# Attention with 16-wide heads: scores and maxima as fp32r pairs in the two row halves of the array, heads streamed in groups of three, TensorE order written out

## The chip, the cores and the metric

The kernel runs on one core of a Trainium2 chip. The metric is the device time of one execution in microseconds (us). The core has TensorE (PE in the profile; PEld is its weight load), VectorE (DVE), ScalarE (ACT), GpSimd (POOL) and SyncE (SP, which only issues DMAs). TensorE writes to PSUM, which has eight banks of 128 x 512 fp32. SBUF is the working memory.

## The reference

Two layers, each made of an attention block and an MLP with Mish, on 2048 tokens of width 512. There are 32 heads of width 16, so the scores of one layer are 32 matrices of 2048 x 2048.

```python
B, S, D, H = 1, 2048, 512, 32
Dh = D // H
q, k, v = qkv[0], qkv[1], qkv[2]
scores = jnp.einsum("bhqd,bhkd->bhqk", q, k) * (Dh ** -0.5)
p = _softmax(scores, axis=-1)
o = jnp.einsum("bhqk,bhkd->bhqd", p, v)
...
x = x + _A_ref(_layernorm(x, axis=-1), A_wqkv, A_wo)
x = x + _B_ref(_layernorm(x, axis=-1), B_w1, B_b1, B_w2)
x = x + _A_ref(_layernorm(x, axis=-1), A_wqkv, A_wo)
x = x + _B_ref(_layernorm(x, axis=-1), B_w1, B_b1, B_w2)
```

## The kernel before

**Stages.** For each layer: layernorm and transposition (`norm_parts`), the projections to q, k and v (`qkv`), the attention (`Attention.run`), the output projection (`wo_parts`), and the MLP (`mlp`). Matmuls with full precision are made of three fp32r matmuls on a high and a low part (`mm3`, L111).

**q and k.** `qkv` splits each 128 x 512 piece of the projected q or k into three bf16 parts (L385 to L388: ACT, DVE, ACT, POOL) and stores them to a scratch tensor in DRAM, with a DMA that ACT issues. `prep_qk` (L187) loads them for a group of four heads, from SP's queue: 16 partitions for each of six products of a part of k with a part of q, so that one matmul over 96 rows gives the score in nearly full precision. Two more rows (to 98) carry ones in k and the negated row maximum in q, so that the score comes out with the maximum already subtracted.

**The attention.** A group has four heads, and a layer eight groups. A group runs over four blocks of 512 queries, and a block over 16 key tiles of 128; a step `s` is one key tile of one block for four heads. There are 512 steps in a layer. In a step:

- `score` (L273), four times: one matmul, keys stationary and 512 queries moving, into one of three PSUM banks (tag "s"); then ACT takes the exponential into SBUF (L287), 512 elements for each partition.
- `max_mm` (L219), four times, for a step 20 later (AHEAD): queries stationary and 512 keys moving, into one half of a two-bank PSUM tile (tag "mx", two buffers, four banks). After every second one DVE reduces 1024 elements to their maximum (L245).
- `pv` (L289) for the step before: four fp32 matmuls, one for each head, to four strips of 32 columns of the array, so that they run at once. They add up in one PSUM bank (tag "acc") over the 16 key tiles.

All eight PSUM banks are in use: three for scores, four for maxima, one for pv. Every 16 steps `max_rows` (L257) transposes the maxima on PE and sends them by eight DMAs into the rows of q, and `out_rows` (L309) transposes the outputs and divides them by the sums. Both take a bank with tag "s" while the loop runs.

**Order.** The order of the matmuls on TensorE is that in which the program lists them: `pe` (L176) ties each to the one before. In a step this is score 0, score 1, three maxima, score 2, one maximum, score 3, the transposes that are due (`tick`), and pv. The 20 steps of maxima that the loop is ahead are done between the last projections (`some_max`, L361). In a layer's last 20 steps no maxima are left, and the first part of the output projection (`wo_first`) goes in their place.

**SBUF.** Most large tiles come from one pool, "blk", of 22 blocks of 8 KB for each partition: k and q of a group (four blocks), v in two forms, the outputs, and the exponentials (one block for each step).

Of the kernel before, what the change touches and what calls it, by code (L numbers as in the profile page):

```python
# [9 lines left out]
F32 = mybir.dt.float32  # L10
# [28 lines left out]
STEPS = NG * GSTEPS  # L39
LAG = 2  # L40
MAX_M = (2, 6, 3, 7)
# [5 lines left out]
def kernel(ctx: ExitStack, tc: tile.TileContext, x, wqkv, wo, w1, b1, w2, out):  # L47
# [16 lines left out]
    nc.gpsimd.memset(lnhalf, LN_HALF)  # L64
    ones = const.tile([MROWS - KROWS, 256], BF16, name="ones")
    nc.gpsimd.memset(ones, 1.0)
# [3 lines left out]
    def b8(shape, dt, name):  # L70
        return blk.tile(shape, dt, tag="blk", name=name)

    def pbank(tag, name):
        return ps.tile([P, 512], F32, tag=tag, name=name, bufs=3 if tag == "s" else 1)

# [86 lines left out]
    class Attention:  # L162
        def __init__(self, l, scr):
            self.l, self.scr = l, scr
            self.vall = {}
            self.qk, self.va, self.mxs, self.pts, self.accs = {}, {}, {}, {}, {}
# [20 lines left out]
        def prep_qk(self, g):  # L187
            l = self.l
            ks, qs = [], []
            for u in range(HG // 2):  # L190
                k = b8([P, 2, S], BF16, f"ks{l}{g}{u}")
                q = b8([P, 2, S], BF16, f"qs{l}{g}{u}")
                nc.sync.dma_start(
                    k[KROWS:MROWS].rearrange("p h (r n) -> p (h r) n", n=256),
                    ones[:, None, :].to_broadcast([MROWS - KROWS, 2 * S // 256, 256]),
                )
                m, h0 = divmod(g * HG + 2 * u, P // DH)
                for t, parts, base in ((k, K_PARTS, NCH), (q, Q_PARTS, 0)):
                    for j, a in enumerate(parts):
                        nc.sync.dma_start(  # L200
                            t[j * DH : (j + 1) * DH],
                            self.scr[base + m][a, h0 * DH : (h0 + 2) * DH, :].rearrange("(h d) n -> d h n", d=DH),
                        )
                ks.append(k)
                qs.append(q)
            self.qk[g] = (ks, qs)
# [11 lines left out]

        def max_mm(self, s, n):  # L219
            if s >= STEPS:  # L220
                return
            b, i = divmod(s, NKT)
            g, qb = divmod(b, NCH)
            h, qt = divmod(i, NCH)
            half, j = divmod(n, 2)
            l = self.l
            if n == 0 and s % GSTEPS == GSTEPS // 2 and g + 1 < NG:
                self.prep_qk(g + 1)
            ks, qs = self.qk[g]
            if i == 0 and n == 0:  # L230
                self.mxs[b] = tmp.tile([P, HG, NCH, 2], F32, tag="mxv", name=f"mxv{l}{b}")
            if j == 0:
                self.pm = ps.tile([P, 2, 512], F32, tag="mx", name=f"pm{l}{b}{i}{half}")
            q0 = qb * CW + qt * P
            self.pe(
                nc.tensor.matmul(  # L236
                    self.pm[:, j],
                    qs[h // 2][0:KROWS, h % 2, q0 : q0 + P],
                    ks[h // 2][0:KROWS, h % 2, ts(n, 512)],
                    start=True,  # L240
                    stop=True,
                )
            )
            if j == 1:
                nc.vector.tensor_reduce(self.mxs[b][:, h, qt, half : half + 1], self.pm, axis=AX.XY, op=ALU.max)  # L245
                if i == NKT - 1 and half == 1:
                    self.max_fold(b)

# [8 lines left out]
        def max_rows(self, b, nm):  # L257
            g, qb = divmod(b, NCH)
            l = self.l
            _, qs = self.qk[g]  # L260
            tp = pbank("s" if self.running else "acc", f"nmt{l}{b}")
            self.pe(nc.tensor.transpose(tp[0 : HG * NCH, 0:P], nm, ident))
            np_ = tmp.tile([HG * NCH, 2, P], BF16, tag="np", name=f"np{l}{b}")
            nc.vector.tensor_copy(np_[:, 0], tp[0 : HG * NCH, 0:P])
            nc.vector.tensor_tensor(np_[:, 1], tp[0 : HG * NCH, 0:P], np_[:, 0], op=ALU.subtract)
            for h in range(HG):
                for a in range(2):
                    nc.sync.dma_start(
                        qs[h // 2][KROWS + a : KROWS + a + 1, h % 2, ts(qb, CW)].rearrange("o (t n) -> o t n", n=P),
                        np_[h * NCH : (h + 1) * NCH, a, :],  # L270
                    )

        def score(self, s, h):  # L273
            b, kt = divmod(s, NKT)
            g, qb = divmod(b, NCH)
            ks, qs = self.qk[g]
            if h == 0:
                self.pts[s] = b8([P, HG, CW], F32, f"p{self.l}{s}")
            sp = pbank("s", f"sc{self.l}{s}{h}")
            self.pe(nc.tensor.matmul(  # L280
                sp,
                ks[h // 2][0:MROWS, h % 2, ts(kt, P)],
                qs[h // 2][0:MROWS, h % 2, ts(qb, CW)],
                start=True,
                stop=True,
            ))
            nc.scalar.activation(self.pts[s][:, h, :], sp, AF.Exp, scale=SCALE)  # L287

        def pv(self, s):  # L289
            b, kt = divmod(s, NKT)  # L290
# [6 lines left out]
            pt = self.pts.pop(s)  # L297
            for h in range(HG):
                self.pe(nc.tensor.matmul(  # L299
                    acc[ts(h, VW), :], va[:, kt, h, :], pt[:, h, :], start=kt == 0, stop=kt == NKT - 1  # L300
                ))
# [23 lines left out]
        def run(self, hooks, ost, fill):  # L325
# [3 lines left out]
            self.running = True  # L329
            for s in range(STEPS):  # L330
                if s % GSTEPS == GSTEPS - NKT and s // GSTEPS + 1 < NG:
                    self.prep_v(s // GSTEPS + 1)
                self.score(s, 0)
                self.score(s, 1)
                for n in range(3):
                    self.max_mm(s + AHEAD, n)
                self.score(s, 2)
                self.max_mm(s + AHEAD, 3)
                if s + AHEAD >= STEPS:
                    next(fill, None)  # L340
                self.score(s, 3)
                self.tick()
                if s:
                    self.pv(s - 1)
                if s in hooks:
                    hooks[s]()
            self.pv(STEPS - 1)
            self.tick(99)

# [7 lines left out]
    def qkv(l, wts, tt, order, late):  # L357
        scr = [dram.tile([3, P, S], BF16, name=f"scr{l}{m}") for m in range(2 * NCH)]
        att = Attention(l, scr)
        ahead = [0]  # L360

        def some_max():
            if ahead[0] < AHEAD:
                att.chained = True
                att.tick()
                for n in range(4):
                    att.max_mm(ahead[0], n)
                ahead[0] += 1

        done = 0  # L370
        for m, c in order:
            if c not in tt:
                late()
            w = wts[m // 2]
            pt = tmp.tile([P, 3, CW], BF16, tag="raw", name=f"pt{l}{m}{c}", bufs=3)
            th, tl = tt[c]
# [9 lines left out]
            nc.vector.tensor_tensor(r, acc, p0, op=ALU.subtract)  # L386
            nc.scalar.activation(p1, r, AF.Copy)
            nc.gpsimd.tensor_tensor(p2, r, p1, op=ALU.subtract)  # L388
            nc.scalar.dma_start(scr[m][:, :, ts(c, CW)].rearrange("a p n -> p a n"), pt)
            if (m, c) == (5, 3) and 4 not in wts:  # L390
# [148 lines left out]
    for l in range(2):  # L539
# [58 lines left out]
        if l == 0:  # L598
            late = lambda: norm(x2s[last], f"q1{last}", tt, last, "mx", True)


# [26 lines left out]
```

## Time and profile before

| | |
|---|---|
| Time, median of 3 runs | 4034.32 us (4033.05 to 4035.47) |
| The profiled execution's span | 4036.3 us |
| PE busy | 3985.8 us (99%) |
| DVE busy | 3075.2 us (76%) |
| ACT busy | 2697.6 us (67%) |
| POOL busy | 568.7 us (14%) |
| DMA | 124.10 MB, 30 GB/s over the span |

The profile is of one execution. In a row of a group of instructions stand the line of the kernel, the engine, the operation, the tiles it writes and reads, shapes and number; then the busy time in us, the mean duration of one in ns, and the idle time of the engine just before them with what ended it. In the rows of a timeline stand the start in us, the time from the first start to the last end, and how many follow each other; in brackets the idle time before. Matmuls are pipelined: a row lasts longer than the time until the next one can start.

### The profile page before, as it was taken

The numbers are of one execution on the slowest core, as the hardware profiler recorded it, in microseconds if no ns is written. First come the engines' busy times: TensorE is split into PE (matmuls) and PEld (weight loads), VectorE is DVE, ScalarE is ACT, GpSimd is POOL, SyncE is SP. The second block draws the span as 40 slices with busy tenths as digits, with TensorE's granted clock in tenths as the row PEclk, the third lists the DMA queues.
The fourth block names the chain that finished last, engine by engine and source line by source line (L and its number), as shares of the span: only waits on it lengthen the run. The fifth ranks groups of instructions, "written<-read, shape, count | busy, mean of one in ns | idle before, by whom it ended". The sixth has DMA issues, their size and how long they took to land.

```text
span 4036.3 us, 54209 instructions
## 1 busy us (share of the span) xinstructions
PE 3985.8 (99%) x21312; PEld 1753.5 (43%) x21312; DVE 3075.2 (76%) x3266; ACT 2697.6 (67%) x4875; POOL 568.7 (14%) x465
## 2 busy tenths in 40 slices
PE   7999999999999999999999999999999999999999
PEld 5733333333333333687766333333333333336887
DVE  5588888888888888566555888888888888875655
ACT  3377777777777777544443777777777777775444
POOL 3200000000000020354431000000000000203545
PEclk9999999999999999999999999999999999999999
DMA  5220120202020200100042110201010201011000
GB/s 167 79 32 11 23 33 1 33 1 33 1 33 1 32 22 32 58 11 11 22 138 78 21 22 12 33 1 32 1 33 1 32 8 26 22 32 58 11 11 22
DMA packets 79535, 124.10 MB, mean 31 GB/s; under 512 B 14256, under 2 KB 51120, under 8 KB 79280
## 3 DMA queue, kind: packets, MB, share of 16 engines
q1 hardware_dynamic: 48848, 88.12, 10.9%
q10 hardware_dynamic: 30432, 32.51, 2.4%
q8 instruction: 168, 2.75, 0.3%
q14 instruction: 87, 0.71, 0.1%
HBM read 85.99 MB, written 33.55 MB: 30 GB/s over the span
## 4 chain that ended last, share of the span: by engine, by line
PE 48%; DVE 3%; POOL 1%; ACT 1%; issue 0%; DMA 0%; POOLq 0%; DVEq 0%; SPq 0%; ACTq 0%
PE pv L299 13%; PE sc L280 12%; PE pm L236 11%; PE mo L116 1%; PE h L114 1%; PE h L116 1%; PE h L115 1%; PE mo L114 1%; PE mo L115 1%; POOL hb L477 1%; DVE al L478 1%; PE qk L114 1%; PE qk L115 1%; POOL hb L474 1%; PE qk L116 1%
## 5 line engine op out<-in xcount | busy, mean ns | idle before, releaser
L245 DVE TENSOR_REDUCE mxv<-pm 128x1 f32<-128x1024 f32 x2048 | 2414.3, 1220 | 512.4 <-PE pm L236 506.5
L287 ACT ACTIVATE p<-sc 128x512 f32<-128x512 f32 x4096 | 2208.1, 596 | 667.3 <-PE sc L280 667.3
L280 PE MATMUL sc<-qs,ks 98*128 98x512 bf16 x4096 | 1390.9, 382 | 0.2
L236 PE MATMUL pm<-ks,qs 96*128 96x512 bf16 x4096 | 1214.4, 379 | 2.7 <-DMA ks<-scr 1.4
L299 PE MATMUL pv<-p,va 128*32 128x512 f32 x8192 | 1090.5, 605 | 0.0
L280 PEld LDWEIGHTS <-ks 98*128 98x128 bf16 x4096 | 314.7, 97 | 1108.4 <-issue 866.4
L236 PEld LDWEIGHTS <-qs 96*128 96x128 bf16 x4096 | 396.4, 98 | 491.5 <-issue 12.9
L210 POOL MEMSET va<- 128x2048 f32 x16 | 28.9, 1806 | 2419.9 <-PE pv L299 2233.4
L299 PEld LDWEIGHTS pv<-p,va 128*32 128x32 f32 x8192 | 161.4, 108 | 406.0 <-issue 385.2
L474 POOL TENSOR_TENSOR hb<-hb,he 128x512 f32<-128x512 f32 x112 | 157.7, 1408 | 186.2 <-DVE he L471 179.3
L477 POOL TENSOR_TENSOR hb<-hb,hr 128x512 f32<-128x512 f32 x112 | 160.9, 1437 | 135.8 <-DVE ah L476 114.5
L114 PE MATMUL mo<-w,ah 128*128 128x512 f32 x448 | 178.9, 399 | 0.7 <-DVE ah L476 0.7
L114 PE MATMUL h<-thm,w 128*128 128x512 f32 x448 | 176.6, 394 | 1.6 <-ACT hb L468 1.6
L115 PE MATMUL mo<-w,ah 128*128 128x512 f32 x448 | 177.1, 395 | 0.0
L472 ACT ACTIVATE hr<-he 128x512 f32<-128x512 f32 x112 | 70.9, 633 | 157.9 <-DVE he L471 79.2
L116 PE MATMUL h<-thm,w 128*128 128x512 f32 x448 | 175.9, 393 | 0.0
L115 PE MATMUL h<-tlm,w 128*128 128x512 f32 x448 | 175.8, 392 | 0.0
L478 DVE TENSOR_TENSOR al<-hb,ah 128x512 fp32r<-128x512 f32 x112 | 111.8, 998 | 83.8 <-POOL hb L477 83.8
L116 PE MATMUL mo<-w,al 128*128 128x512 f32 x448 | 163.2, 401 | 7.5 <-DVE al L478 7.5
L470 ACT ACTIVATE he<-he 128x512 f32<-128x512 f32 x112 | 70.8, 632 | 102.0 <-DVE he L469 99.0
L476 DVE TENSOR_TENSOR ah<-hb,hr 128x512 fp32r<-128x512 f32 x112 | 76.9, 686 | 62.5 <-ACT hr L473 42.9
L114 PE MATMUL qk<-thq,wqk 128*128 128x512 f32 x256 | 110.6, 434 | 7.9 <-DVE pr L386 4.4
(167 smaller groups left out, 2637.8 us busy)
## 6 DMA issues: line engine op xcount, KB each, us to landing
scr<-pt ACTq DMA_DIRECT2D x64, 384.0 KB
qs<-scr SPq DMA_DIRECT2D x192, 128.0 KB
ks<-scr SPq DMA_DIRECT2D x192, 128.0 KB
qs<-np SPq DMA_DIRECT2D x512, 1.0 KB
x<-in_A_x_dram SPq DMA_DIRECT2D x7, 1024.0 KB
xs<-x SPq DMA_DIRECT2D x4, 1024.0 KB
x<-xs SPq DMA_DIRECT2D x4, 1024.0 KB
out_dram<-x SPq DMA_DIRECT2D x3, 1024.0 KB
```

Source lines behind the costliest of these rows:

```text
L114: pe(nc.tensor.matmul(acc, ah, bh, start=first and i == 0, stop=False))
L115: pe(nc.tensor.matmul(acc, ah, bl, start=False, stop=False))
L116: pe(nc.tensor.matmul(acc, al, bh, start=False, stop=last and i == n - 1))
L236: nc.tensor.matmul(self.pm[:, j], qs[h // 2][0:KROWS, h % 2, q0 : q0 + P], ks[h // 2][0:KROWS, h % 2, ts(n, 512)], start=True, stop=True,)
L245: nc.vector.tensor_reduce(self.mxs[b][:, h, qt, half : half + 1], self.pm, axis=AX.XY, op=ALU.max)
L280: self.pe(nc.tensor.matmul(sp, ks[h // 2][0:MROWS, h % 2, ts(kt, P)], qs[h // 2][0:MROWS, h % 2, ts(qb, CW)], start=True, stop=True,))
L287: nc.scalar.activation(self.pts[s][:, h, :], sp, AF.Exp, scale=SCALE)
L299: self.pe(nc.tensor.matmul(acc[ts(h, VW), :], va[:, kt, h, :], pt[:, h, :], start=kt == 0, stop=kt == NKT - 1))
L474: nc.gpsimd.tensor_tensor(hb, hb, e, op=ALU.mult)
L476: nc.vector.tensor_tensor(ah, hb, r, op=ALU.mult)
L477: nc.gpsimd.tensor_tensor(hb, hb, r, op=ALU.mult)
L478: nc.vector.tensor_tensor(al, hb, ah.bitcast(F32), op=ALU.subtract)
```

## The change

- q and k are split into two fp32r parts instead of three bf16 parts (one ACT and one DVE instruction for each piece). Three products of parts are left, so a head needs 48 rows, and 50 with the two for the maximum. Two heads of a pair stand in one tile, at partitions 0 to 49 and 64 to 113.
- `max_mm` issues two matmuls, for the two heads of a pair on the same 512 keys, one in each half of the rows, each into a bank of the "mx" tile. DVE reduces both at once to two maxima. There are two such pairs in a step instead of four single matmuls, and as many reductions.
- Scores are no longer made step by step, but head by head in groups of three: `pair` fills a tile of two banks (tag "s2") with two heads and takes one exponential of 1024 elements; `single` fills one bank (tag "s1") and takes one of 512. Each has one buffer. The exponentials of three heads share one block of the pool.
- The order in three steps is written out in CYCLE: P is `pair`, S is `single`, M is a pair of `max_mm`, V is `pv`, which now runs two steps behind.
- `max_rows` and `out_rows` take a "mx" tile. The three score banks are in a pool of their own, which is closed for the loop and opened again behind it.

```diff
-KROWS = 96
-MROWS = 98
-K_PARTS = (0, 0, 0, 1, 1, 2)
-Q_PARTS = (0, 1, 2, 0, 1, 0)
+KROWS = 48
+MROWS = 50
+HALF = 64
+K_PARTS = (0, 0, 1)
+Q_PARTS = (0, 1, 0)
+CYCLE = ("PSMV", "PMSMPV", "SMPMSMV")
...
+    def open_banks():
+        banks["pool"] = tc.tile_pool(name="sp", bufs=1, space=PSUM, reuse_waits="tile")
+        banks["s"] = banks["pool"].__enter__()
...
     def pbank(tag, name):
-        return ps.tile([P, 512], F32, tag=tag, name=name, bufs=3 if tag == "s" else 1)
+        if tag == "s":
+            return banks["s"].tile([P, 512], F32, tag=tag, name=name, bufs=3)
+        return ps.tile([P, 512], F32, tag=tag, name=name, bufs=1)
...
-                k = b8([P, 2, S], BF16, f"ks{l}{g}{u}")
-                q = b8([P, 2, S], BF16, f"qs{l}{g}{u}")
...
+                k = b8([P, S], F32R, f"ks{l}{g}{u}")
+                q = b8([P, S], F32R, f"qs{l}{g}{u}")
                 m, h0 = divmod(g * HG + 2 * u, P // DH)
...
+                for e in range(2):
+                    r0 = e * HALF
+                    nc.sync.dma_start(
+                        k[r0 + KROWS : r0 + MROWS].bitcast(F32).rearrange("p (r n) -> p r n", n=256),
+                        ones[:, None, :].to_broadcast([MROWS - KROWS, S // 256, 256]),
+                    )
+                    for t, parts, base in ((k, K_PARTS, NCH), (q, Q_PARTS, 0)):
+                        for j, a in enumerate(parts):
+                            nc.sync.dma_start(
+                                t[r0 + j * DH : r0 + (j + 1) * DH].bitcast(F32),
+                                self.scr[base + m][a, (h0 + e) * DH : (h0 + e + 1) * DH, :].bitcast(F32),
+                            )
...
-        def max_mm(self, s, n):
+        def max_mm(self, s, half):
...
+            pm = ps.tile([P, 2, 512], F32, tag="mx", name=f"pm{l}{b}{u}{i}")
             q0 = qb * CW + qt * P
...
+            for e in range(2):
+                rows = slice(e * HALF, e * HALF + KROWS)
+                self.pe(
+                    nc.tensor.matmul(
+                        pm[:, e], qs[u][rows, q0 : q0 + P], ks[u][rows, ts(n, 512)], start=True, stop=True
+                    )
                 )
...
+            nc.vector.tensor_reduce(self.mxs[b][:, 2 * u : 2 * u + 2, qt, n], pm, axis=AX.X, op=ALU.max)
...
-            tp = pbank("s" if self.running else "acc", f"nmt{l}{b}")
+            tp = ps.tile([P, 2, 512], F32, tag="mx", name=f"nmt{l}{b}")[:, 0]
...
+        def head_rows(self, i):
+            s, h = divmod(i, HG)
             b, kt = divmod(s, NKT)
             g, qb = divmod(b, NCH)
             ks, qs = self.qk[g]
...
+            rows = slice(h % 2 * HALF, h % 2 * HALF + MROWS)
+            return ks[h // 2][rows, ts(kt, P)], qs[h // 2][rows, ts(qb, CW)]
+
+        def pair(self):
+            i = 3 * len(self.pts)
+            n = min(2, HEADS - i)
+            if n <= 0:
+                return
+            sp = self.pool.tile([P, 2, CW], F32, tag="s2", name=f"sp{self.l}{i}")
+            self.pts.append(b8([P, 3, CW], F32, f"p{self.l}{i}"))
+            for e in range(n):
+                k, q = self.head_rows(i + e)
+                self.pe(nc.tensor.matmul(sp[:, e], k, q, start=True, stop=True))
+            nc.scalar.activation(self.pts[-1][:, 0:n], sp[:, 0:n], AF.Exp, scale=SCALE)
+
+        def single(self):
+            i = 3 * self.singles + 2
+            self.singles += 1
+            if i >= HEADS:
+                return
+            sp = self.pool.tile([P, CW], F32, tag="s1", name=f"ss{self.l}{i}")
+            k, q = self.head_rows(i)
+            self.pe(nc.tensor.matmul(sp, k, q, start=True, stop=True))
+            nc.scalar.activation(self.pts[i // 3][:, 2], sp, AF.Exp, scale=SCALE)
...
-            tp = pbank("s", f"otp{l}{b}")
+            tp = ps.tile([P, 2, 512], F32, tag="mx", name=f"otp{l}{b}")[:, 0]
...
+            close_banks()
+            with tc.tile_pool(name="sa", bufs=1, space=PSUM, reuse_waits="tile") as self.pool:
+                half, done = 2 * AHEAD, -2
+                for s in range(STEPS + 2):
...
+                    for item in CYCLE[s % 3]:
+                        if item == "P":
+                            self.pair()
+                        elif item == "S":
+                            self.single()
+                        elif item == "M":
+                            self.max_mm(half // 2, half % 2)
+                            half += 1
+                        else:
+                            self.pv(done)
+                            done += 1
+                    if s + AHEAD >= STEPS:
+                        next(fill, None)
+                    self.tick()
...
+            open_banks()
...
-            p0, p1, p2 = (pt[:, a] for a in range(3))
-            r = t512("f", f"pr{l}{c}{m}")
-            nc.scalar.activation(p0, acc, AF.Copy)
-            nc.vector.tensor_tensor(r, acc, p0, op=ALU.subtract)
-            nc.scalar.activation(p1, r, AF.Copy)
-            nc.gpsimd.tensor_tensor(p2, r, p1, op=ALU.subtract)
...
+            split_psum(pt[:, 0], pt[:, 1], acc)
```

More of the change, by code (lines that the diff above doesn't have):

```diff
@@ L64 @@
     nc.gpsimd.memset(lnhalf, LN_HALF)
-    ones = const.tile([MROWS - KROWS, 256], BF16, name="ones")
+    ones = const.tile([MROWS - KROWS, 256], F32, name="ones")
     nc.gpsimd.memset(ones, 1.0)
@@ L223, in max_mm @@
             g, qb = divmod(b, NCH)
-            h, qt = divmod(i, NCH)
-            half, j = divmod(n, 2)
+            u, i = divmod(2 * i + half, GSTEPS // 4)
+            qt, n = divmod(i, NCH)
             l = self.l
-            if n == 0 and s % GSTEPS == GSTEPS // 2 and g + 1 < NG:
+            if half == 0 and s % GSTEPS == GSTEPS // 2 and g + 1 < NG:
                 self.prep_qk(g + 1)
             ks, qs = self.qk[g]
[L230 to L233, printed above, removed]
+            if u == 0 and i == 0:
+                self.mxs[b] = tmp.tile([P, HG, NCH, NCH], F32, tag="mxv", name=f"mxv{l}{b}")
+            pm = ps.tile([P, 2, 512], F32, tag="mx", name=f"pm{l}{b}{u}{i}")
             q0 = qb * CW + qt * P
[L235 to L241, printed above, removed]
-                )
[L243 to L247, printed above, removed]
+            for e in range(2):
[4 more added lines that the diff above has]
+                    )
+                )
+            nc.vector.tensor_reduce(self.mxs[b][:, 2 * u : 2 * u + 2, qt, n], pm, axis=AX.X, op=ALU.max)
+            if u == 1 and i == GSTEPS // 4 - 1:
+                self.max_fold(b)
         def max_fold(self, b):
@@ L276, in score @@
             ks, qs = self.qk[g]
[L277 to L287, printed above, removed]
+            rows = slice(h % 2 * HALF, h % 2 * HALF + MROWS)
[20 more added lines that the diff above has]
+            nc.scalar.activation(self.pts[i // 3][:, 2], sp, AF.Exp, scale=SCALE)
         def pv(self, s):
+            if not 0 <= s < STEPS:
+                return
             b, kt = divmod(s, NKT)
@@ L296, in pv @@
             acc = self.accs[b]
-            pt = self.pts.pop(s)
             for h in range(HG):
+                j, e = divmod(s * HG + h, 3)
                 self.pe(nc.tensor.matmul(
-                    acc[ts(h, VW), :], va[:, kt, h, :], pt[:, h, :], start=kt == 0, stop=kt == NKT - 1
+                    acc[ts(h, VW), :], va[:, kt, h, :], self.pts[j][:, e, :], start=kt == 0, stop=kt == NKT - 1
                 ))
@@ L329, in run @@
             self.running = True
[L330 to L348, printed above, removed]
+            close_banks()
+            with tc.tile_pool(name="sa", bufs=1, space=PSUM, reuse_waits="tile") as self.pool:
+                half, done = 2 * AHEAD, -2
+                for s in range(STEPS + 2):
+                    if s % GSTEPS == GSTEPS - NKT and s // GSTEPS + 1 < NG:
+                        self.prep_v(s // GSTEPS + 1)
+                    for item in CYCLE[s % 3]:
[12 more added lines that the diff above has]
+                    self.tick()
+                    if s in hooks:
+                        hooks[s]()
+                self.tick(99)
+            open_banks()
     def load_qkv(l, wts, which, **kw):
@@ L357, in qkv @@
     def qkv(l, wts, tt, order, late):
-        scr = [dram.tile([3, P, S], BF16, name=f"scr{l}{m}") for m in range(2 * NCH)]
+        scr = [dram.tile([2, P, S], F32R, name=f"scr{l}{m}") for m in range(2 * NCH)]
         att = Attention(l, scr)
@@ L365, in some_max @@
                 att.tick()
-                for n in range(4):
+                for n in range(2):
                     att.max_mm(ahead[0], n)
```

35 lines of the change are left out of this document (17 added, 18 removed).

## The prediction

> **What bounds the kernel now.** I read the page first: busy time, granted clock, and the costliest groups.
>
> ```profile
> span 4036.3 us, 54209 instructions
> ...
> PE 3985.8 (99%) x21312; PEld 1753.5 (43%) x21312; DVE 3075.2 (76%) x3266; ACT 2697.6 (67%) x4875; POOL 568.7 (14%) x465
> ...
> PEclk9999999999999999999999999999999999999999
> ...
> L245 DVE TENSOR_REDUCE mxv<-pm 128x1 f32<-128x1024 f32 x2048 | 2414.3, 1220 | 512.4 <-PE pm L236 506.5
> L287 ACT ACTIVATE p<-sc 128x512 f32<-128x512 f32 x4096 | 2208.1, 596 | 667.3 <-PE sc L280 667.3
> L280 PE MATMUL sc<-qs,ks 98*128 98x512 bf16 x4096 | 1390.9, 382 | 0.2
> L236 PE MATMUL pm<-ks,qs 96*128 96x512 bf16 x4096 | 1214.4, 379 | 2.7 <-DMA ks<-scr 1.4 <-DVE mxv L245 1.3
> L299 PE MATMUL pv<-p,va 128*32 128x512 f32 x8192 | 1090.5, 605 | 0.0
> ```
>
> ACT and DVE wait for TensorE (PE) and PE hardly waits for them: 0.2 and 2.7 us over 4096 instructions each. Then busy time by stage, and the first and last score matmul of each layer:
>
> ```profile
> 195.00:1609.00 1414.00, 1413.50 (x8025) 438.83 (x8023) 1196.64 (x1136) 1079.17 (x2002) 44.10 (x55) 1.00 0.12 21
> 1609.00:1661.00 52.00, 51.94 (x305) 20.34 (x309) 13.25 (x21) 40.73 (x80) 7.12 (x3) 1.00 0.07 22
> ...
> 2215.00:3618.00 1403.00, 1403.00 (x7974) 435.39 (x7966) 1188.55 (x1129) 1070.45 (x1986) 43.69 (x54) 1.00 0.12 20
> ```
> ```profile
> L280 PE MATMUL sc<-qs,ks x2048: 376/380/393, 195.4 to 1659.6; 98*128 98x512 bf16 x187
> ```
> ```profile
> L280 PE MATMUL sc<-qs,ks x2048: 376/380/393, 2204.7 to 3668.9; 98*128 98x512 bf16 x187
> ```
>
> Columns of the stage rows: stretch, its length, busy us of PE, weight loads, DVE, ACT and POOL, clock. The two attention stretches are 2 x 1464.2 us, 73% of the span, with PE full and its clock at 1.00. Before 1609 a layer runs 492 steps with four score, four maximum and four pv matmuls; in the last 20 there are no maxima left. One step in order of time, with the start of the next two:
>
> ```profile
> 1000.42 0.38 PE L280 MATMUL sc<-qs,ks 98*128 98x512 bf16 x1
> 1000.73 0.16 PEld L299 LDWEIGHTS pv<-p,va 128*32 128x32 f32 x8 [0.43 <-issue]
> 1000.73 1.07 PE L299 MATMUL pv<-p,va 128*32 128x512 f32 x8
> 1001.73 0.11 PEld L280 LDWEIGHTS <-ks 98*128 98x128 bf16 x2 [0.84 <-issue]
> 1001.73 0.60 PE L280 MATMUL sc<-qs,ks 98*128 98x512 bf16 x2
> ...
> 1002.16 2.17 ACT L287 ACTIVATE p<-sc 128x512 f32<-128x512 f32 x4 [0.67 <-PE sc L280]
> 1002.17 0.81 PE L236 MATMUL pm<-ks,qs 96*128 96x512 bf16 x3
> ...
> 1002.81 2.36 DVE L245 TENSOR_REDUCE mxv<-pm 128x1 f32<-128x1024 f32 x2 [0.48 <-PE pm L236]
> ...
> 1004.57 0.60 PE L280 MATMUL sc<-qs,ks 98*128 98x512 bf16 x2
> ```
>
> A step is 1004.57 - 1001.73 = 2.83 us, so three are 8.50. Rows overlap: a bf16 matmul lasts 0.38 but the next starts 0.22 later (1001.73 to 1002.17 is two). From the last row before pv to the first after it are 1000.42 to 1001.73 = 1.31 us. The eight pv weight loads, to four column strips, take 0.16 together where one takes 0.11: loads to different parts of the array overlap here. Two reductions take 2.36, so they follow at 2.36 - 1.22 = 1.14. DVE therefore needs 2.28 per step.
>
> **The change, part by part.** Pairs: scores and maxima of two heads go to rows 0-63 and 64-127 as fp32r. Nothing in this trace shows two row halves at work, only column strips. Bounds: a pair costs one slot, or two. I take one, by the nearest row (pv's strips). The pitch of fp32r, and what it costs when it has waited, come from the MLP:
>
> ```profile
> 1980.02 0.68 ACT L468 ACTIVATE hb<-h,b1t 128x512 f32<-128x512 f32 x1
> ...
> 1980.76 0.19 PEld L114 LDWEIGHTS h<-thm,w 128*128 128x128 f32 x1 [0.76 <-ACT hb L468]
> 1980.76 0.50 PE L114 MATMUL h<-thm,w 128*128 128x512 f32 x1 [0.33 <-ACT hb L468]
> ...
> 1981.34 0.40 PE L116 MATMUL h<-thm,w 128*128 128x512 f32 x1
> 1981.34 0.19 PEld L114 LDWEIGHTS h<-thm,w 128*128 128x128 f32 x1
> ...
> 1981.57 0.40 PE L114 MATMUL h<-thm,w 128*128 128x512 f32 x1
> ```
>
> Pitch 0.23. Normally the load (0.19) hides under the matmul before it. But this matmul needed only its PSUM bank back from ACT, and its weight load waited too: ACT ends at 1980.70, the load starts 0.06 later, and the matmul row grows from 0.39 to 0.50. So an fp32r matmul that waits for a bank shows 0.11 of its load; the bf16 ones did not. After pv the load is not pulled ahead either (the 0.84 above), so fp32r adds 0.11 there too. PE to ACT takes 0.04 (1001.73 + 0.39 to 1002.16).
>
> Exponentials of 1024 elements; the nearest rows are 512 and 1024 from SBUF:
>
> ```profile
> L470 ACT ACTIVATE he<-he 128x512 f32<-128x512 f32 x112 | 70.8, 632 | 102.0 <-DVE he L469 99.0
> ...
> L89 ACT ACTIVATE w<-w216r 128x1024 fp32r<-128x1024 f32 x1 | 1.1, 1063 | 2.5 <-DMA w216r<-in_B_w_dram 2.5
> ```
>
> The second 512 add 0.43, so from PSUM 0.60 + 0.43 = 1.02 (two separate would be the other end, 1.19).
>
> Now the waits. Every score bank has one buffer and each P (pair), S (single) or M (maximum pair) stands in a fixed PE order, PSMV PMSMPV SMPMSMV; what waits on PE holds all behind it. Around these three steps I added, from each link to the next:
> - first P to second P of the middle step: matmuls 0.40, to ACT 0.04, exponential 1.02, back 0.05, load 0.11 = 1.62;
> - second P over V to the S behind it: 1.31 + 0.01 (pitch) + 0.11 = 1.43; S to M 0.24;
> - that M to the third M, which needs its buffer: 0.40 + 0.04 + 1.22 + 0.05 + 0.11 = 1.82;
> - over V to P 1.43, to S 0.22, to M 0.24, over V to the next first P 1.43.
>
> The whole walk, each item at the later of PE free and its bank free, from that first P: P 0, M 0.23, S 0.46, M 0.69, P 1.62; V; S 3.05, M 3.28, P 3.52, M 3.75, S 4.23 (behind two exponentials), M 5.10; V; P 6.54, S 6.76, M 7.00; V; P 8.43. All other items find their banks free.
>
> Sum 1.62 + 1.43 + 0.24 + 1.82 + 1.43 + 0.22 + 0.24 + 1.43 = **8.43 us** against 8.50. PE's four halved slots are spent on two waits that did not exist and on 5 x 0.11 of exposed loads. Over 984 steps (2 x 492) that is 984 x 0.07 / 3 = -23 us.
>
> What lies around it:
>
> ```profile
> 937.02 0.38 PE L280 MATMUL sc<-qs,ks 98*128 98x512 bf16 x1
> ...
> 937.24 0.60 PE L314 MATMUL otp<-ident,ot 128*128 128x128 f32 x4
> 937.77 0.16 PEld L299 LDWEIGHTS pv<-p,va 128*32 128x32 f32 x8 [0.17 <-issue]
> ```
>
> The output transposes cost 937.77 - 937.02 - 0.31 = 0.44 today. They keep the whole array, so now it changes shape twice more. A change costs 0.31 - 0.22 = 0.09 (sc to pv), the first pair behind pays 0.11: 0.29 a visit, two visits (maxima's rows, outputs) in 16 steps, 61.5 times: +36 at most, 0 if a wait hides it; they also take a maximum buffer in turn, so I take +30. In the 20 steps without maxima, 52 us now, pairs save about 0.16 a step and the output projection's visits add 0.30: +6. The first 20 maxima steps, between projections: 4 x 0.22 before, 2 x 0.23 + 0.30 now: -4 in two layers.
>
> The q/k split loses one ACT pass, one POOL pass, and each store grows from 384 to 512 KB; loads stay 128 KB each, and 28 instead of 26 a group stand in SP's queue, ahead of the row writes of the maxima.
>
> ```profile
> L114 PE MATMUL qk<-thq,wqk 128*128 128x512 f32 x256 | 110.6, 434 | 7.9 <-DVE pr L386 4.4 <-ACT thq L108 3.5
> ```
> ```profile
> scr<-pt ACTq DMA_DIRECT2D x64, 384.0 KB
> qs<-scr SPq DMA_DIRECT2D x192, 128.0 KB
> ks<-scr SPq DMA_DIRECT2D x192, 128.0 KB
> ```
>
> PE waits there 7.9 us in all, and 1.4 for loads (first fence): between -8 and some us, taken as 0; PE's own projections cover it, as do 32 steps between a group's loads and their first use. Swapping the score banks' pools: 0 to about 1 us, four times, +2. P tiles hold three heads in a 22-block pool; counting blocks (18 long-lived in the last 16 steps of a group) I find 5 wanted and 4 free once in three steps. The exponential then waits for V; the third M's wait mostly covers that. 0 to 75 x 0.6 = 45, taken as +5.
>
> Sum: -23 + 30 + 6 - 4 + 2 + 5 = +16 on the execution of 4036.3. That one stands 2 us above the median of 4034.3, so **4050 us**.
>
> One rule speaks against the change. The Trainium skill, "TensorE: Matmul & The Clock Gate", Part 3, says that a weight load overlaps running matmuls only where their row groups differ. The rows above differ for the full array: the load at 1981.34 runs beside a matmul on the same rows. No row here shows it for halves.
>
> **Rivals.**
> 1. *Loads covered (faster).* If a pair's weights are loaded before its bank is free, the 5 x 0.11 go: 8.43 - 0.55 = 7.88, or 0.21 a step, -203; visits cost 0.18 each, +22 instead of +30: 4034 - 203 + 31 = **3865**. Against: the load at 1980.76 waited. It turns the sign once less than about 0.09 of the 0.11 is exposed.
> 2. *DVE becomes the bound (faster).* If the waits stagger better than in my walk, DVE's 2.28 and about 0.09 of small operations remain, 2.37 against 2.87 (2.83 and the transposes): about **3550**. Against: two maximum buffers and one per score bank.
> 3. *Loads in a half are not hidden at all (slower).* Then six further slots of the walk pay 0.11: 9.09, 3.03 a step, +194, and +39 around: **4265**. For: nothing shows loads under matmuls in halves. By the skill's rule just named it would come out so.
> 4. *The halves do not overlap (the change does not do what it says).* Each pair adds 0.22 to the walk six times: 9.75, 3.25 a step, +410 + 39: **4485**. Against: pv's strips overlap.
>
> **From cases to numbers.** My walk 45% (its own range 3990 to 4110, from 0.05 a step either way); rival 1 17%, 2 6%, 3 18%, 4 12%, others 2%. The range 3780 to 4300 leaves out rivals 2 and 4. What the measurement can tell from no change is about 0.2%, 8 us. Of the walk's 45, 15 are faster, 8 within, 22 slower, as its terms almost cancel. Faster: 15 + 17 + 6 + 1 = 39%; same 8%; slower 22 + 18 + 12 + 1 = 53%.
>
> **What would show it.** Right: the two matmuls of a pair start within 0.02 us; three steps take 8.4; PE, no longer full, waits for ACT at one P in three steps and for DVE at one M, each with a 0.50 row; DVE and ACT stay below 90% busy. Wrong: rows of 0.39 behind a wait (rival 1); DVE without gaps (2); 0.34 between pairs (3); 0.23 between the halves of a pair (4).

## The result, and the profile after

| | before | after |
|---|---|---|
| Median of the runs side by side | 4033.69 us (4030.27 to 4035.47) | 4234.77 us (4228.51 to 4237.53) |
| Span of the profiled execution | 4036.3 us | 4230.5 us |

The changed kernel is slower: ratio 1.0499 [1.0485, 1.0514], 201 us more. The forecast was 4050 and the range 3780 to 4300: the direction came true, the size (16 us forecast) did not. First the page of the changed kernel:

```profile
span 4230.5 us, 53996 instructions
...
PE 3790.1 (90%) x21312; PEld 1893.5 (45%) x21312; DVE 3083.0 (73%) x3266; ACT 2528.0 (60%) x3445; POOL 495.3 (12%) x401
...
PEclk9999799999999999999999999999999999999999
...
L261 DVE TENSOR_REDUCE mxv<-pm 128x2 f32<-128x1024 f32 x2048 | 2421.6, 1221 | 650.9 <-PE pm L257 546.2
L308 ACT ACTIVATE p<-sp 128x1024 f32<-128x1024 f32 x1366 | 1399.7, 1025 | 836.3 <-PE sp L307 727.1
```

PE is no longer full, DVE and ACT fill a smaller share of the span than before, and one digit of the clock is a 7. No engine has become the bound. What PE waits for says more (engine, line, releaser, sum, times, longest):

```profile
PE sp L307 <- ACT p L308: 181.5, 376, 1.0
PE pm L257 <- DVE mxv L261: 97.8, 263, 0.6
PE sp L307 <- DMA qs<-np: 63.1, 8, 9.2
PE ss L317 <- DMA qs<-np: 37.3, 19, 7.8
```

The first two are the waits of the forecast's walk. The other two, 100.4 us with a longest of 9.2, are not in the forecast: a score waits for the row maxima (`np`), which `max_rows` (L273) writes into q by DMA. And the clock, as a mean over the span, before and then after:

```profile
core 0: 4036.3 us, clock 0.996
```
```profile
core 0: 4230.5 us, clock 0.969
```

The clock's records in both traces hold only the values 1.00 and 0.50, so a mean of 0.969 is 2 x 0.031 x 4230.5 = 262 us at half clock, against 2 x 0.004 x 4036.3 = 32 before.

**Three quiet steps**, away from those waits, in the timeline of the changed kernel:

```profile
997.84 0.50 PE L307 MATMUL sp<-qs,ks 50*128 50x512 f32 x2 [0.15 <-ACT p L308]
998.27 1.06 PE L332 MATMUL pv<-p,va 128*32 128x512 f32 x8
...
1001.32 0.50 PE L257 MATMUL pm<-ks,qs 48*128 48x512 f32 x2 [0.37 <-DVE mxv L261]
1001.75 1.06 PE L332 MATMUL pv<-p,va 128*32 128x512 f32 x8
...
1003.64 1.06 PE L332 MATMUL pv<-p,va 128*32 128x512 f32 x8
...
1004.74 0.19 PEld L257 LDWEIGHTS pm<-ks,qs 48*128 48x128 f32 x2
1004.97 0.40 PE L257 MATMUL pm<-ks,qs 48*128 48x512 f32 x2
1004.97 0.19 PEld L317 LDWEIGHTS ss<-qs,ks 50*128 50x128 f32 x1
...
1005.20 0.39 PE L317 MATMUL ss<-qs,ks 50*128 50x512 f32 x1
...
1006.31 0.50 PE L307 MATMUL sp<-qs,ks 50*128 50x512 f32 x2 [0.48 <-ACT p L308]
1006.74 1.07 PE L332 MATMUL pv<-p,va 128*32 128x512 f32 x8
```

From pv to pv: 1001.75 - 998.27 = 3.48, then 1.89, then 3.10: 8.47 us for three steps. One wait is for DVE at an M, one for ACT at a P, and the rows behind them last 0.50. Two matmuls of a pair take 0.40 together where one takes 0.39, so they start within 0.01.

**A boundary between two groups of heads**, 560 us earlier:

```profile
431.81 1.06 PE L332 MATMUL pv<-p,va 128*32 128x512 f32 x8
440.66 0.76 PE L317 MATMUL ss<-qs,ks 50*128 50x512 f32 x1 [7.78 <-DMA qs<-np]
...
443.98 1.93 PE L332 MATMUL pv<-p,va 128*32 128x512 f32 x8
...
447.42 1.93 PE L332 MATMUL pv<-p,va 128*32 128x512 f32 x8
```
```profile
444.00:490.00 46.00, 45.01 (x177) 16.50 (x176) 25.10 (x24) 21.61 (x29) 0.00 (x0) 0.53 0.00 0
500.00:546.00 46.00, 41.40 (x263) 16.48 (x255) 38.74 (x38) 33.34 (x45) 0.00 (x0) 1.00 0.01 1
```

PE waits 7.78 us, and then pv takes 1.93 instead of 1.06. The two stretches of 46 us (busy us and matmuls of PE first, clock third from the end) show why: the clock is 0.53 and 177 matmuls are done, against 263 at 1.00. A mean of 0.53 is 43.2 of the 46 us at half clock, so each us at half clock with PE at work loses (1 - 177/263) x 46 / 43.2 = 0.35. The wait itself as a stretch:

```profile
432.88:440.66 7.78, 0.00 (x0) 0.03 (x1) 0.00 (x0) 0.13 (x1) 0.00 (x0) 0.71 0.58 82
```

Its mean clock of 0.71 says that for 4.5 of the 7.78 us the clock is at a half already, while PE stands still and loses nothing by it.

**Where the 194 us of the two spans went.** From the starts of pv in both traces, both layers together:

```
steps of a layer      before    after
pv 0 to 64             366.7    374.9    +8.3
pv 64 to 448          2205.3   2364.2  +158.9   six group boundaries a layer
pv 448 to 490          241.4    241.7    +0.3   maxima, but no boundary
pv 490 to 511          108.6    133.0   +24.3   no maxima left
outside                                  +2.4
```

The twelve waits of over 6 us at boundaries sum to 92.5. The clock's records show 208.2 us at half clock around them, of which 55.6 lie inside the waits; the other 152.6, at 0.35, cost about 53. Together that is 146 of the 159. Most of the rest is spread over all blocks: 16 steps without a long wait or half clock take 46.2 us on average against 45.9 before, which is 11 in 48 blocks. The 8.3 of the first row are 23 us at half clock at the start of the two layers, and no wait for rows stands before those.

**Why the maxima come late.** What SP issues around that boundary (start, length of the issues), after and before; L214, L220 and L193, L200 are `prep_qk`, L285 and L268 the rows of the maxima:

```profile
412.58 0.69 SPq L214 DMA_DIRECT2D ks<-ones  x1
413.32 1.32 SPq L220 DMA_DIRECT2D ks<-scr  x3
...
433.23 1.89 SPq L220 DMA_DIRECT2D qs<-scr  x3
435.92 5.78 SPq L285 DMA_DIRECT2D qs<-np  x8
```
```profile
396.13 0.68 SPq L193 DMA_DIRECT2D ks<-ones  x1
...
409.60 3.95 SPq L200 DMA_DIRECT2D qs<-scr  x6
416.63 5.05 SPq L268 DMA_DIRECT2D qs<-np  x8
```

After, DVE has the rows ready at 428.7, but SP is still issuing the loads of the next group, until 435.12: the rows start 7.2 us late. Before, the loads were all issued at 413.55, and SP then waited for the rows. Two things moved. The first load waits for a free block of the pool, which a pv frees, the pv of a layer's step 68 before and of step 70 now (and of each 64th step after these), which also runs two steps behind instead of one. So the loads start 11.0 to 16.1 us ahead of the rows instead of 20.8, at the six boundaries of each layer. And their issue takes longer, 20.7 to 22.8 us instead of 16.6 to 19.9. The same stretches as windows, after and before:

```profile
412.00:435.00 23.00, 18.68 (x120) 7.07 (x114) 17.80 (x18) 15.33 (x21) 0.00 (x0) 1.00 0.94 126
```
```profile
396.00:414.00 18.00, 18.00 (x105) 5.58 (x102) 14.88 (x14) 13.54 (x26) 0.00 (x0) 1.00 0.90 145
```

In both, the DMA engines are busy (0.94, 0.90), but they move 126 GB/s instead of 145. From 16.1 down to 11.0 against some 22 the rows are 5 to 12 us late, which is what the traces show at every boundary.

### The profile page after: what moved, and what is told of

The parts are those of the page before. It is cut to its first block, busy times and chain, and to the rows that moved or that the text cites. A ratio compares the mean times of both kernels' runs of the same rounds, so it can differ in the third digit from the quotient of the medians.

```text
span 4230.5 us, 53996 instructions
## 1 busy us (share of the span) xinstructions
PE 3790.1 (90%) x21312; PEld 1893.5 (45%) x21312; DVE 3083.0 (73%) x3266; ACT 2528.0 (60%) x3445; POOL 495.3 (12%) x401
## 4 chain that ended last, share of the span: by engine, by line
PE 34%; DVE 6%; ACT 6%; DMA 4%; POOL 1%; issue 1%; SPq 1%; ACTq 0%; DVEq 0%; POOLq 0%
PE pv L332 11%; PE sp L307 5%; ACT p L308 4%; DVE mxv L261 4%; PE pm L257 4%; PE ss L317 2%; DMA qs<-scr 2%; PE mo L133 1%; PE h L131 1%; PE h L133 1%; PE h L132 1%; PE mo L131 1%; PE mo L132 1%; DMA ks<-ones 1%; DMA qs<-np 1%
## 5 line engine op out<-in xcount | busy, mean ns | idle before, releaser
L261 DVE TENSOR_REDUCE mxv<-pm 128x2 f32<-128x1024 f32 x2048 | 2421.6, 1221 | 650.9 <-PE pm L257 546.2
L308 ACT ACTIVATE p<-sp 128x1024 f32<-128x1024 f32 x1366 | 1399.7, 1025 | 836.3 <-PE sp L307 727.1
L257 PE MATMUL pm<-ks,qs 48*128 48x512 f32 x4096 | 1105.9, 436 | 100.7 <-DVE mxv L261 97.8
L332 PE MATMUL pv<-p,va 128*32 128x512 f32 x8192 | 1121.8, 621 | 0.0
L307 PE MATMUL sp<-qs,ks 50*128 50x512 f32 x2732 | 744.5, 488 | 246.1 <-ACT p L308 181.5
L318 ACT ACTIVATE p<-ss 128x512 f32<-128x512 f32 x1364 | 809.9, 594 | 152.6 <-PE pm L257 134.9
L307 PEld LDWEIGHTS sp<-qs,ks 50*128 50x128 f32 x2732 | 296.6, 188 | 926.6 <-ACT p L308 560.3
L257 PEld LDWEIGHTS pm<-ks,qs 48*128 48x128 f32 x4096 | 581.5, 191 | 263.8 <-DVE mxv L261 207.9
L317 PE MATMUL ss<-qs,ks 50*128 50x512 f32 x1364 | 615.3, 451 | 45.6 <-DMA qs<-np 37.3
L317 PEld LDWEIGHTS ss<-qs,ks 50*128 50x128 f32 x1364 | 259.4, 190 | 454.4 <-issue 286.5
```

What stands on the lines that cost most here:

```text
L257: nc.tensor.matmul(pm[:, e], qs[u][rows, q0 : q0 + P], ks[u][rows, ts(n, 512)], start=True, stop=True)
L261: nc.vector.tensor_reduce(self.mxs[b][:, 2 * u : 2 * u + 2, qt, n], pm, axis=AX.X, op=ALU.max)
L307: self.pe(nc.tensor.matmul(sp[:, e], k, q, start=True, stop=True))
L308: nc.scalar.activation(self.pts[-1][:, 0:n], sp[:, 0:n], AF.Exp, scale=SCALE)
L317: self.pe(nc.tensor.matmul(sp, k, q, start=True, stop=True))
L318: nc.scalar.activation(self.pts[i // 3][:, 2], sp, AF.Exp, scale=SCALE)
```

## The experiments

All are edits of the changed kernel. Theory: the rows stand behind the loads on SP, and the rest of the loss is the half clock behind that wait. The rivals were that the row halves or the waits of the written-out order are the cause, that the DMA engines and not SP's queue hold the rows back, and that the number of live exponential blocks sets the start of the loads.

**1. The loads four steps later**, so that the rows go first.

```diff
-            if half == 0 and s % GSTEPS == GSTEPS // 2 and g + 1 < NG:
+            if half == 0 and s % GSTEPS == GSTEPS // 2 + 4 and g + 1 < NG:
```

> The loads of the next group's k and q are issued four maxima steps later, so that they stand behind the row writes of the maxima on SP's queue and not ahead of them; nothing else changes. Queue theory (the row writes were ready 7 us before SP reached them; the score matmul waited for them, and the clock fell to a half after it): the twelve waits of 7 to 9 us and the stretches of half clock behind them go, the blocks of 16 steps at a group's boundary take 46.6 us instead of 55 to 59, and the time falls by about 140 us to 4095 (4080 to 4115). Rival, the loads themselves are the limit (DMA engines or late k and q): the wait moves to the first maxima of the next group and the time stays above 4200. Rival, the clock halves because PE is no longer dense, not because of the wait: waits go but half clock stays, about 4140.

Measured: 4096.05 us (4086.35 to 4099.43), ratio 1.0152 [1.0137, 1.0167]. SP's order, the waits of PE and the clock:

```profile
422.51 4.96 SPq L285 DMA_DIRECT2D qs<-np  x8
427.58 0.69 SPq L214 DMA_DIRECT2D ks<-ones  x1
```
```profile
PE sp L307 <- ACT p L308: 191.0, 385, 1.6
PE pm L257 <- DVE mxv L261: 97.6, 263, 0.6
PE ss L317 <- DMA qs<-np: 10.8, 19, 1.5
```
```profile
core 0: 4097.6 us, clock 0.990
```

The wait for the rows falls from 100.4 to 10.8 us and the clock rises to 0.990: one moved start gives back 139 of the 201 us. The walk's own waits stay (191.0 and 97.6), so they are not what cost the 139. About 63 us over before remain: 24 in the last steps of the layers, 10.8 for rows, a half clock of 82 - 32 = 50 us, worth 17, and some 10 in the blocks of 16 steps, which take 46.1 us instead of 45.9 even without long waits and half clock. Most of that half clock stands behind a smaller wait, in the same trace:

```profile
992.49 0.60 ACT L339 ACTIVATE ot<-pv 128x512 f32<-128x512 f32 x1 [2.66 <-PE pv L332]
992.98 1.02 ACT L308 ACTIVATE p<-sp 128x1024 f32<-128x1024 f32 x1
...
994.05 0.50 PE L307 MATMUL sp<-qs,ks 50*128 50x512 f32 x2 [1.63 <-ACT p L308]
...
996.46 1.94 PE L332 MATMUL pv<-p,va 128*32 128x512 f32 x8
```

The copy of the outputs (L339) waits on ACT for the end of pv. An exponential whose scores were there by 990.96 stands behind it, PE waits 1.63 us for the bank, and two us later pv takes 1.94. Four such waits are in this trace, each with a half clock behind it. That they cause it is read from the order in time alone: in experiment 8 the waits of 1.63 us at 403.93 and 2859.77 leave the clock at 1.00.

**2. The rows on POOL's queue**, with the loads as in the changed kernel.

```diff
-                    nc.sync.dma_start(
+                    nc.gpsimd.dma_start(
                         qs[h // 2][r : r + 1, ts(qb, CW)].bitcast(F32).rearrange("o (t n) -> o t n", n=P),
```

> The row writes of the maxima are issued from POOL's queue; the loads of k and q stay where they were on SP's. Queue theory: they no longer stand behind the loads, the waits go, 4080 to 4120. Rival, what delays them is the traffic of the loads on the shared DMA engines: they still land late, above 4180.

Measured: 4212.86 us (4203.4 to 4225.18), ratio 1.0456 [1.0438, 1.0474]: what the rival expected. POOL and PE in its timeline:

```profile
426.11 4.08 POOL L285 DMA_DIRECT2D qs<-np  x8 [46.08 <-DVE np L280]
```
```profile
436.41 0.76 PE L317 MATMUL ss<-qs,ks 50*128 50x512 f32 x1 [6.12 <-DMA qs<-np]
```

The rows are issued as soon as they are ready, all by 430.19, and still PE gets them 6.2 us later, while the last loads were issued until 432.6. So SP's queue is only one place where the rows are held: they also land late while the DMA engines are full of loads. POOL's queue is not slow in itself: a row takes 7.6 to 8.3 us from issue to landing here, and 1.6 to 2.6 us at the next rows, issued from 479.3 on with no loads under way. Experiment 1 had put them ahead of the loads in both places and could not tell the two apart. The wait for rows falls only from 100.4 to 58.4 us (28.8 and 29.6).

**3. Packets of 4096 bytes** as before, instead of 8192: each row of the scratch tensor in two halves.

```diff
-        scr = [dram.tile([2, P, S], F32R, name=f"scr{l}{m}") for m in range(2 * NCH)]
+        scr = [dram.tile([2, 2, P, S // 2], F32R, name=f"scr{l}{m}") for m in range(2 * NCH)]
```

> The changed kernel with the scratch tensor in two halves of the tokens, so that a load of q or k moves in 32 packets of 4096 bytes as in the kernel before and not in 16 of 8192; same bytes, same number of DMAs, same order. Packet theory (16 packets leave the DMA engines unevenly filled, so the 28 loads take 24 us and not 20): the loads end about 4 us earlier, each of the twelve waits is 3 to 4 us shorter, 4150 to 4190. Rival, only the late start matters: within 10 us of 4235.

Measured: 4214.19 us (4206.59 to 4241.94), ratio 1.046 [1.0424, 1.0497]: slower than expected, and faster than the rival. In a stretch of loads:

```profile
409.00:429.00 20.00, 17.82 (x114) 6.76 (x110) 17.02 (x17) 14.49 (x19) 0.00 (x0) 1.00 0.94 139
```

139 GB/s instead of 126 at this boundary, but over all boundaries the issue still takes 18.8 to 22.3 us. The packets are a small part; what else makes 28 loads slower than 26 stays open.

**4. pv one step behind** instead of two, so that blocks come free sooner.

```diff
-                half, done = 2 * AHEAD, -2
-                for s in range(STEPS + 2):
+                half, done = 2 * AHEAD, -1
+                for s in range(STEPS + 1):
```

> The changed kernel with pv one step behind, as in the kernel before, and not two; the order and the place of the loads are those of the change. Lag theory (SP's first load of a group waits for the block of an exponential that pv gives back, and pv now runs a step later): the loads start one step, about 2.9 us, earlier against the rows of the maxima (17 to 19 us ahead instead of 14.6 to 16), the waits at a group's boundary shrink by as much, and with less half clock the time falls to 4150 to 4190. Rival, the start is set by something else: loads start as in the changed kernel, 4210 or more.

Measured: 4194.24 us (4183.13 to 4208.33), ratio 1.0402 [1.0377, 1.0427], just above the expectation. The loads start 14.5 to 18.0 us ahead of the rows instead of 11.0 to 16.1, released by the same pv of step 70, and the long waits are 3.8 to 6.2 us instead of 6.6 to 9.2. So the distance of pv makes 1.9 to 3.5 of the 4.7 to 9.8 us by which the loads start later than before.

**5. Another order of the matmuls alone**, loads as in the changed kernel. In it no exponential waits for V to free a block of the pool, where the changed kernel has 50 such waits.

```diff
-CYCLE = ("PSMV", "PMSMPV", "SMPMSMV")
+CYCLE = ("MPMSV", "PMSV", "MPSMVPMS")
```

> The changed kernel with the order of e5_order2 alone; the loads of the next group stay ahead of the row writes. In this order at most four blocks of exponentials are alive, not five. Block theory (the loads start late, 16 us before the rows are ready where the kernel before starts them 21 us before, because they wait for a block that pv gives back later): the loads start at least 3 us earlier against the rows and the waits of 7.7 us shrink to under 5; about 3920. Rival, the start does not depend on the blocks: waits as long as in the changed kernel or longer, since the steps are shorter, 4000 or more.

Measured: 4007.49 us (3972.81 to 4030.52), ratio 0.9927 [0.9894, 0.996], 0.7% below the kernel before. The loads did not start sooner (10.3 to 14.6 us ahead of the rows) and the long waits stayed (3.6 to 10.1). The theory that the number of live blocks sets the start falls. The gain is that of the order, which experiment 7 has without these waits.

**6. Experiment 1 with one V moved**, one M behind it:

```diff
-CYCLE = ("PSMV", "PMSMPV", "SMPMSMV")
+CYCLE = ("PSMV", "PMSMPV", "SMPMSVM")
```

> As e1_prep_later, and in the written order one M is moved behind the V that it stood ahead of (the third step SMPMSVM). Walk theory (three steps are the sum of two waits on banks and three passages over pv): the third M no longer waits for DVE, three steps take 7.8 us instead of 8.45, the time falls by another 200 us to about 3890 (3850 to 3940), below the kernel before. Rival, the pair's fixed latencies do not set the pace: 8.3 or more, above 4040.

Measured: 3962.19 us (3955.24 to 3969.91), ratio 0.9825 [0.9809, 0.984]: 1.7% below the kernel before, which is less than expected. Undisturbed blocks of 16 steps take 42.7: 16/3 of the expected 7.8 is 41.6, and the visits of the transposes (maxima's rows, outputs) would add about the 1.1 that the forecast has for the changed kernel. But many blocks take 43 to 47, and what holds those up was not traced.

**7. Experiment 1 with the order of experiment 5.**

> As e1_prep_later, with the order MPMSV PMSV MPSMVPMS, the best that the walk gives when every item starts at the later of PE free and bank free. Walk theory: three steps take about 7.7 us, 3870 (3820 to 3930), and one block of the pool less is alive. Rival, waits that the walk leaves out (row writes, transposes, blocks) take over: no better than e4_order.

Measured: 3870.96 us (3858.96 to 3891.93), ratio 0.9604 [0.9572, 0.9635], as expected. It beats both kernels by the order and the start of the loads alone. PE's waits in it:

```profile
PE sp L307 <- ACT p L308: 120.0, 304, 1.6
PE pm L257 <- DVE mxv L261: 13.6, 22, 2.8
```

The wait for DVE goes from 97.6 to 13.6 and that for ACT from 191.0 to 120.0. Three steps take 1.90 + 2.13 + 3.73 = 7.76.

**8. Experiment 1 with q, k and the rows of the maxima in two bf16 parts** instead of two fp32r parts. The scores are less exact, the loads half as large; order and number of the matmuls stay.

```diff
-                k = b8([P, S], F32R, f"ks{l}{g}{u}")
-                q = b8([P, S], F32R, f"qs{l}{g}{u}")
+                k = b8([P, S], BF16, f"ks{l}{g}{u}")
+                q = b8([P, S], BF16, f"qs{l}{g}{u}")
...
-            np_ = tmp.tile([HG * NCH, 2, P], F32R, tag="np", name=f"np{l}{b}", bufs=1)
+            np_ = tmp.tile([HG * NCH, 2, P], BF16, tag="np", name=f"np{l}{b}", bufs=1)
```

> As e1_prep_later, but q and k and the maxima's rows are split into two bf16 parts instead of two fp32r parts, in the same rows, so the scores are less exact and the loads of q and k half as large. A bf16 matmul's weights are loaded while it still waits for its bank. Walk theory (the 0.11 us of a weight load show at five places in three steps): three steps take 7.85 us instead of 8.48 and the time falls from 4096 to about 3900 (3850 to 3950). Rival, the pace is set by the round over banks and pv alone: 4060 or more.

Measured: 3880.81 us (3879.12 to 3885.2), ratio 0.9623 [0.9609, 0.9637], as expected. The first matmuls of a pair behind a wait:

```profile
1008.10 0.39 PE L307 MATMUL sp<-qs,ks 50*128 50x512 bf16 x2 [0.55 <-ACT p L308]
```

0.39 where the fp32r row had 0.50: the 0.11 of exposed load is a matter of fp32r, and 215 us less than experiment 1 goes with it. Not all of the 215 is exposed load: stores and loads are smaller too (the loads' issue takes 13 to 15 us, and the first pv starts 17 us sooner), and the clock is nearly full.

**9. Experiments 7 and 8 together**, again with less exact scores.

> e6_bf16 (two bf16 parts, loads behind the row writes) with the order of e5_order2; scores are less exact than with fp32r parts. Walk theory: both gains add, 2.50 us a step, 3735 (3700 to 3790). Rival, DVE's reductions (2.28 us a step and its small operations) and the small waits take over: no better than 3830.

Measured: 3677.36 us (3665.46 to 3687.52), ratio 0.9115 [0.909, 0.9141], better than expected. DVE in it:

```profile
L261 DVE TENSOR_REDUCE mxv<-pm 128x2 f32<-128x1024 f32 x2048 | 2380.7, 1218 | 190.4 <-PE pm L257 190.0
```

Its gaps for PE are down to 190 us from 546 in the changed kernel.

## Why the prediction was right or wrong

**The step that failed is the term for the split and the loads**, "between -8 and some us, taken as 0", with PE's projections and "32 steps between a group's loads and their first use" as its cover. It measured about 146 us: 92.5 of waits and about 53 of half clock behind them. The sentence itself named what is late, 28 loads "ahead of the row writes of the maxima", and then priced only the loads. Their 32 steps are some 90 us of cover, and PE's waits for loads sum to at most 3 us in any trace. The rows have their own due time: the next block's scores need them some four us after they are ready (428.7, and PE's wait begins at 440.66 - 7.78 = 432.88). The margin was to be read in the trace of before: loads issued by 413.55, rows issued at 416.63, so 3 us were left (0.7 to 3.9 at the twelve boundaries), and each of the change's edits to the loads' start (a pv two steps behind, another use of the pool's blocks) and to their length had to be held against those 3 us. Moving the loads alone (experiment 1) gives back 139 us, which shows the cause; experiment 2 adds that SP's queue and the traffic of the loads both hold the rows back, without a measure of either share.

**A wait's price was taken as its length.** Nothing in the sum allowed for the clock. Before, PE had no gap in the attention and a clock of 1.00 there. Outside it that trace does show a price: PE waits 2.27 us until 2064.80 and 0.74 us until 2066.19, and the clock is 0.50 from 2066.2 to 2076.5. After, 92.5 us of waits had 153 us at half clock behind them. The Trainium skill, "TensorE: Matmul & The Clock Gate", Part 1, says that an idle window of about 3.4 us halves the clock and about 3.4 us of busy matmuls restore it. The trace agrees with the first for the waits of 6.6 to 9.2 us: the half clock sets in 1.4 to 4.0 us after each begins. With the second it agrees at best in part: the half clock lasts 5.2 to 6.4 us behind five of the twelve waits, but 9.5 to 47 us behind the others, and after 444.00 PE was busy for 45 of 46 us at a clock of 0.53. Nor does experiment 1 fit, where a wait of 1.63 us went before a half clock.

**The walk was right**: 8.43 predicted, 8.47 measured, with the two waits, their places and the rows of 0.50 as described. In bf16 the row behind a wait lasts 0.39, so the 0.11 was right as well. The order of experiment 7 then shows that the walk is a matter of choice: the same work takes 7.76.

**The visits of the transposes were nearly right.** The 16-step blocks without a long wait or half clock have a mean of 46.2 us against 45.9 before; the walk gives 16 x 8.43 / 3 = 44.96, the visits as they were 45.9 - 16 x 2.83 = 0.6, and the +30 over 61.5 times 0.49: 46.0. The 0.2 between them is what three steps of 8.47 instead of 8.43 add up to in 16.

**The last 20 steps were mis-sized**: +6 predicted for both layers, +24.3 measured. The sum took their matmuls and forgot that the two score tiles still have one buffer each. PE's waits in the first layer's last steps (1705 to 1770) in the changed kernel:

```profile
PE sp L307 <- ACT p L308: 6.7, 7, 1.0
PE ss L317 <- ACT p L318: 2.7, 6, 0.5
```

With no M between them, a P waits for the exponential of the P before and an S for that of the S before: 9.4 us a layer and 18.8 in two, which are the 18 that were missing.

**Small terms.** The exponentials that wait for V to free a block were put at "0 to 75 x 0.6 = 45, taken as +5". The trace has 50 such waits with 57.3 us on ACT, and the blocks of 16 steps in which they fall are no longer than others, so little of it reached PE. The stages outside the attention and the swap of the pools came to +2.4 where the forecast had about -2.

**The rivals.** 1 (loads covered): refuted for fp32r by the rows of 0.50, and it is what bf16 does. 2 (DVE the bound): not here; the order that takes its wait away comes nearer to it. 3 (loads in a half not hidden): refuted. At 1004.97 the weight load of an S runs beside two matmuls that fill both halves, and its matmul starts at 1005.20, the usual 0.23 later. The Trainium skill, "TensorE: Matmul & The Clock Gate", Part 3, in the sentence that the prediction cited, would not have let that load run there; these rows do not agree with it. The measured 4235 lies near this rival's 4265 by chance, and inside the range by the same luck. 4 (the halves don't overlap): refuted by 0.40 for two. Two of the prediction's sums are off, and neither matters here: 4034 - 203 + 31 for rival 1 is 3862 and not 3865, and 0.05 a step over 984 steps is 49 us, so the walk's own range would have been 4001 to 4099 and not 3990 to 4110.

**Left open.** Which use of the pool's blocks makes the loads wait for step 70 and not for 68 was not settled (experiments 4 and 5 take away two candidates); why 28 loads move at a lower rate than 26 was settled only for the packets' small part; and when a wait of 1.63 us brings a half clock, and how long the half clock lasts, follow no rule that these traces show.

## What to carry to other kernels

When a change adds to a queue or moves the start of what stands in it, the price isn't read from the work that was added but from the due time of the smallest thing behind it: look up how many us that one had to spare before the change. Where PE is full, a new gap costs its length and a stretch of half clock behind it, which here added some 53 us to 92.5. And in an order written out by hand with single buffers the waits can be worked out beforehand (8.43 us against 8.47 in three steps, though many blocks of experiment 6 ran longer than its walk), so several orders should be walked before one is built.

## What the hardware showed that was not expected

- A wait of PE of 6.6 to 9.2 us was followed by 5 to 47 us at half clock with PE at work, and in experiment 1 waits of 1.63 us by 3 to 24 us, while two such waits in experiment 8 and the waits of 0.95 us in a layer's last steps left the clock at 1.00.
- An fp32r matmul that waited for its bank shows 0.11 us of its weight load (0.50 instead of 0.39), a bf16 one of the same shape doesn't (0.39).
- Rows of 2 KB, issued on another queue, landed 7.6 to 8.3 us after their issue while loads of 128 KB were under way, and after 1.6 to 2.6 us when none were.
